# Attention scores in one plain float32 product per head, in place of three split products

## The chip, the cores and the metric

The kernel runs on one core of one Trainium2 chip. The metric is the device time of one execution in microseconds (us), lower is better. The program is one launch: an attention with mixed heads, followed by two mixtures of dense layers that read its output. A trace of one profiled execution shows, for each engine of the core, when each instruction started, how long it lasted and what its engine had waited for. TensorE is called PE (its weight loads are shown apart, as PEld), VectorE is DVE, ScalarE is ACT, GpSimd is POOL, and SyncE, which issues nearly all transfers, is SP.

## The reference

Only the first lines matter here; the rest of the program follows on the attention's output.

```python
q, k, v = float32 (4, 12, 448, 64)       # batch, heads, positions, head size
scale = 1.0 / 8.0
scores = scale * np.matmul(q, k.transpose(0, 1, 3, 2))
scores = np.einsum('bhij,hg->bgij', scores, w_pre)
scores = scores - np.max(scores, axis=-1, keepdims=True)
attn = np.exp(scores)
attn = attn / (np.sum(attn, axis=-1, keepdims=True) + 1e-09)
attn = np.einsum('bhij,hg->bgij', attn, w_post)
out = np.matmul(attn, v)
```

The output, as 1792 rows of 768, goes through a dense layer pair (768 to 2048 and back, with ELU) and then through a routed layer of 8 experts. Neither of these is touched.

## The kernel before, in words

**Tiles and steps.** `attention` works on 16 query tiles (4 batches of 448 rows, each cut into 120, 120, 120 and 88 rows). Heads go in 6 pairs p; the two heads of a pair lie on partitions 0 to 63 and 64 to 127 of the query and key tiles. The main loop (L397) has 48 steps n, three for each tile. A step mixes, exponentiates and mixes back a third of tile n // 3, multiplies a third of the tile before by the values, and makes the scores of two pairs of heads for the tile T = (n + 5) // 3, so the scores run about two tiles ahead of their use. The scores of tile 0 and of four pairs of tile 1 are made ahead of the loop.

**What each engine does in a step, in the order written.** The order of every engine is that of the program text (a manual schedule), so an instruction that waits holds up all that is behind it on its engine.

- PE: `mix_pre` twice (L204: 16 records of matmul on 64-by-64 quarters of the array), `mix_post` of the first unit of the step before (L264, 64 small matmuls), `av` (L286 and L292, 32 matmuls), `qk` for two pairs of heads (L164), `mix_post` of the second unit (64 matmuls).
- ACT: the rounded copy of the queries (`high_q`, L141), four exponentials with row sums (L225), a copy of `mix_post`'s result (L270), in some steps a rounded copy of keys (`split_k`, L135), the first head of each pair out of PSUM (L168), and two more copies (L270).
- DVE: four row maxima (L212), the remainder of the queries (`low_q`, L145), a copy (L270), the reciprocals of the row sums (L239 and L240), a copy of the `av` result (L302), the second head of each pair (L169).
- POOL: in some steps the remainder of the keys (`split_k`, L136), then the mixing weights scaled by the reciprocals (L245).
- SP: the moves of scores into the layout that mixing wants (`relayout`, L196), stores of the result, loads of queries, keys and values for later tiles (L120, L124, L129).

**The scores.** `qk(T, p)` takes two PSUM banks, one for each head, out of a ring of four (`ps_w`, shared with `mix_pre`). For the first two tiles (T < PLAIN = 2) it multiplies the queries by the keys as they were loaded, in float32. From the third tile on it uses split operands: each number as a rounded high part (float32r) and a remainder, and three products, high by high, high by low, low by high (`THREE`), summed in PSUM. In the loop's order over the three products, the two heads alternate:

```python
for i, (a, z) in enumerate(THREE if T >= PLAIN else ()):
    for ab, ps in enumerate(pss):
        rows = slice(ab * 64, (ab + 1) * 64)
        nc.tensor.matmul(out=ps[:PR, :S], lhsT=qt[T, p // 2][rows, a, p % 2, :], rhs=kt[b, p][rows, z, :],
                         start=(i == 0), stop=(i == 2))
```

**Splitting.** `high_q` and `low_q` split a third of a query tile in each step from n = 1 to n = 42. `split_k` splits the keys of one pair; it runs twice a step in steps 0 to 2 (batch 0, remainder on DVE) and in three steps for each later batch (n = 6 to 8, 18 to 20, 30 to 32, remainder on POOL): 24 times in all. The buffers: raw queries 2, raw keys 6 (one size for all pairs), split queries 3, split keys 1 for each pair.

**After the scores.** From n = 43 on no scores are made, their pools are closed, and the first parts of `mixtures` are put between the attention's last steps. Everything after some 345 us is `mixtures`.

Of the kernel before, what the change touches and what calls it, by code (L numbers as in the profile page):

```python
# [8 lines left out]
FP32 = mybir.dt.float32  # L9
FP32R = mybir.dt.float32r  # L10
# [3 lines left out]
ALU = mybir.AluOpType  # L14
# [4 lines left out]
B, H, S, D = 4, 12, 448, 64  # L19
NT, DM, DFF = B * S, H * D, 2048  # L20
NK = DM // 128
# [8 lines left out]
PR = 120  # L30
# [7 lines left out]
NA = WHOLE * H + NK  # L38
ORDER = [2 * p + (p + s) % 2 for s in range(2) for p in range(NK)]
SCALE = 1.0 / 8.0  # L40
PLAIN = 2
THREE = ((0, 0), (0, 1), (1, 0))


# [36 lines left out]
def attention(tc, q, k, v, w_pre, w_post, xT, mix, ident):  # L81
# [11 lines left out]
    nc = tc.nc  # L93
    with ExitStack() as ctx, ExitStack() as mixing, ExitStack() as scoring:
        pool = lambda name, bufs, ctx=ctx, **kw: ctx.enter_context(tc.tile_pool(name=name, bufs=bufs, **kw))
# [5 lines left out]
        x_p = pool("a_x", 3)  # L101
        d_p = pool("a_d", 1, mixing)
        s_p = [pool("a_s0", 1, scoring, side="right"), pool("a_s1", 1, mixing)]
        k_p = pool("a_k", 1, scoring, side="right")
        rk_p = pool("a_rk", 6, scoring, side="right")
        rq_p = pool("a_rq", 2, scoring, side="right")
        q_p = pool("a_q", 3, scoring, side="right")
        ps_f = pool("ps_f", 2, space=PSUM)
        ps_x = pool("ps_x", 1, space=PSUM)
        ps_w = pool("ps_w", 4, mixing, space=PSUM, side="right")  # L110

        tiles = [(b, it) for b in range(B) for it in range(len(ROWS))]
        raw_q, raw_k, vt, kt, qt, st, att = {}, {}, {}, {}, {}, {}, {}

        def load_q(T, us=None):
            b, it = tiles[T]
            if T not in raw_q:
                raw_q[T] = rq_p.tile([128, NK, PR], FP32, tag="rq", name="rq")
            for p0, p1 in us or [(0, NK)]:
                nc.sync.dma_start(out=raw_q[T][:, p0:p1], in_=q[b, :, it, p0:p1])  # L120

        def load_k(b, p):
            raw_k[b, p] = rk_p.tile([128, S], FP32, tag="rk", name="rk")
            nc.sync.dma_start(out=raw_k[b, p], in_=k[b, p])  # L124

        def load_v(b, p):

            vt[b, p] = v_p.tile([128, 2 * WHOLE + 1, D], FP32, tag=f"v{p}", name="v")
            nc.sync.dma_start(out=vt[b, p].rearrange("s r d -> s (r d)"), in_=v[b, p])  # L129

        def split_k(b, p, eng):

            t = kt[b, p] = k_p.tile([128, 2, S], FP32R, tag=f"k{p}", name="k")
            raw = raw_k.pop((b, p))
            nc.scalar.copy(out=t[:, 0], in_=raw)  # L135
            eng.tensor_tensor(out=t[:, 1], in0=raw, in1=t[:, 0], op=ALU.subtract)  # L136

        def high_q(T, u):

            t = qt[T, u] = q_p.tile([128, 2, 2, PR], FP32R, tag="q", name="qq")  # L140
            nc.scalar.copy(out=t[:, 0], in_=raw_q[T][:, 2 * u:2 * u + 2])  # L141

        def low_q(T, u):
            t = qt[T, u]
            nc.vector.tensor_tensor(out=t[:, 1], in0=raw_q[T][:, 2 * u:2 * u + 2], in1=t[:, 0], op=ALU.subtract)  # L145

        def split_q(T, u):
            high_q(T, u)
            low_q(T, u)

        def qk(T, p):

            b = tiles[T][0]
            if p == 0:
                st[T] = s_p[T % 2].tile([128, H, S], FP32, tag="s", name="s")
            pss = [ps_w.tile([128, 512], FP32, tag="w", name="qk") for _ in range(2)]
            for ab, ps in enumerate(pss):
                rows = slice(ab * 64, (ab + 1) * 64)
                if T < PLAIN:
                    nc.tensor.matmul(out=ps[:PR, :S], lhsT=raw_q[T][rows, p, :], rhs=raw_k[b, p][rows, :])  # L160
            for i, (a, z) in enumerate(THREE if T >= PLAIN else ()):
                for ab, ps in enumerate(pss):
                    rows = slice(ab * 64, (ab + 1) * 64)
                    nc.tensor.matmul(out=ps[:PR, :S], lhsT=qt[T, p // 2][rows, a, p % 2, :], rhs=kt[b, p][rows, z, :],  # L164
                                     start=(i == 0), stop=(i == 2))

            def move():
                nc.scalar.activation(out=st[T][:PR, 2 * p, :], in_=pss[0][:PR, :S], func=ACTF.Copy, scale=SCALE)  # L168
                nc.vector.tensor_scalar(out=st[T][:PR, 2 * p + 1, :], in0=pss[1][:PR, :S], scalar1=SCALE, scalar2=None,  # L169
                                        op0=ALU.mult)  # L170
            return move
# [13 lines left out]
        def relayout(U):  # L185

            dr[U] = {}
            for j, G in enumerate(U):
                T, r, m = blks[G]
                whole = ROWS[tiles[T][1]][1] // BR * BR  # L190
                t = r // BR if r < whole else (whole // BR) + (r - whole) // m
                rows = st[T][:PR].rearrange("(a t) h s -> t a h s", a=BR)[t][:m]
                t = d_all[n_d[0] % ND]
                n_d[0] += 1
                half = m // 2 * H
                nc.sync.dma_start(out=t[UP - half:UP + half, :], in_=rows)  # L196
                dr[U][0, j], dr[U][1, j] = t[:UP], t[UP:UP + HP]
# [31 lines left out]
        def softmax(U):  # L229
            for e in exps(U):  # L230
                e()
# [79 lines left out]
        def store():  # L311
            for to, x in stores:
                nc.sync.dma_start(out=to, in_=x)
            stores.clear()
# [28 lines left out]
        def when(n):  # L343

            return n // 3, n % 3


        warm = const.tile([128, 128], FP32, name="warm")
        nc.vector.memset(warm, 0.0)
        load_q(0, [(0, 2)])  # L350
        load_k(0, 0)
        load_k(0, 1)
# [15 lines left out]
        ps = ps_f.tile([128, 512], FP32, tag="f", name="f")  # L368
# [3 lines left out]
        for p in range(NK):  # L372
# [11 lines left out]
            if p == 3:  # L384
                nc.vector.tensor_copy(out=kposts[1][:HP].rearrange("p (g i) -> p g i", g=H),
                                      in_=kpost[:HP].rearrange("p (g i) -> p g i", g=H)[:, :, :HR])
# [10 lines left out]
        for n in range(NP):  # L397
            cur, old = units[n], units[n - 1] if n else ()
            new = units[n + 1] if n + 1 < NP else ()
            T, u = when(n + 5)  # L400
            T1, u1 = when(n + 6)
            T2, u2 = when(n + 7)
            for U in new[1:]:
                relayout(U)
            store()
            if n == NP - 5:
                scoring.close()
            late = n >= NP - 5
            for bp in values[:2] if n else ():
                load_v(*bp)  # L410
            del values[:2 if n else 0]
            if T2 < len(tiles):
                if u2 == 0:
                    load_q(T2)
                if tiles[T2][1] == 0:
                    load_k(tiles[T2][0], 2 * u2)
                    load_k(tiles[T2][0], 2 * u2 + 1)
            if PLAIN <= T < len(tiles):
                high_q(T, u)
            for i, U in enumerate(cur):  # L420
                mix_pre(U)
                if i == 0 and n + 2 < NP:
                    relayout(units[n + 2][0])
            for U in cur:
                top(U)
            if PLAIN <= T < len(tiles):
                low_q(T, u)
            softmax(cur[0])
            moves, scores = [mix_post(U) for U in old[:1]], []
            weighted = [av((n - 1) // 3 - 1, (n - 1) % 3)] if n >= 4 else []  # L430
            if T < len(tiles):
                scores.append(qk(T, 2 * u))
            if not late:
                for U in cur[1:]:
                    softmax(U)
            for m in moves:
                m[1](nc.scalar.copy)
                m[0](nc.vector.tensor_copy)
            if late:
                for U in cur[1:]:  # L440
                    softmax(U)
                next(mix)
            keys = (tiles[T1][0], 2 * u1, nc.gpsimd) if T1 < len(tiles) and tiles[T1][1] == 0 else ()
            if n < 3:
                keys = 0, 2 * n, nc.vector
            if keys:
                split_k(*keys)
            if late:
                next(mix)
            norm(cur)  # L450
            for f in weighted:
                f()
            if T < len(tiles):
                scores.append(qk(T, 2 * u + 1))
            for f in scores:
                f()
            if keys:
                split_k(keys[0], keys[1] + 1, keys[2])
            moves = [mix_post(U) for U in old[1:]]
            if late:  # L460
                next(mix)
            for m in moves:
                m[1](nc.scalar.copy)
                m[0](nc.scalar.copy)
            if n == NP - 1:
                av(n // 3 - 1, n % 3)()
            if late:
                next(mix)
# [903 lines left out]
```

## Time and profile before

| what | value |
|---|---|
| median of 3 runs | 1002.85 us (1000.85 to 1008.06) |
| profiled execution | 1004.38 us, of which the span of its trace is 1002.6 us |
| busy share of the span | PE 98%, weight loads 85%, DVE 72%, ACT 55%, POOL 24% |
| granted clock of TensorE over the span | 0.992 of full speed (2.4 GHz) |
| plain score products (L160), 48 records of matmul | 15.3 us busy |
| split score products (L164), 504 records of matmul | 67.0 us busy |
| mixing ahead of softmax (L204), 736 records of matmul | 166.9 us busy, in two groups that run side by side |

The span is the time from the first to the last instruction in the trace; the execution's own time is 1.78 us longer. A busy time of a group is the time in which at least one of its instructions ran, so for matmuls that run side by side it is less than count times duration. The recorded duration of a matmul includes its way through the array, so successive matmuls overlap in the records, and what one costs is read from the distance between starts.

### The profile page before, as it was taken

Reading aid. Unit: us, or ns where it says so; the run is one execution under the profiler, and the core shown is the slowest. Engines: PE = TensorE matmul, PEld = TensorE weight load, DVE = VectorE, ACT = ScalarE, POOL = GpSimd, SP = SyncE. Lnnn points to the kernel's source line nnn. Section 1 sums busy time; section 2 is a strip of 40 time slices with the busy share of each in tenths; the row PEclk is TensorE's granted clock in tenths of the full one; section 3 lists DMA queues with packets and bytes.
Section 4 is the critical chain, followed back from the end, with each engine's and each line's share of the span. In section 5 each row is a group of like instructions: output and inputs, shape, how many; then the busy total and the mean of one; then the engine's idle time right before and its main releaser. Section 6 shows DMA issues by size and latency. Waiting matters only on the chain. (4 is left out here: it accounts for less than half of the span.)

```text
span 1002.6 us, 29974 instructions
## 1 busy us (share of the span) xinstructions
PE 979.3 (98%) x12216; PEld 855.5 (85%) x12216; DVE 725.1 (72%) x1462; ACT 553.3 (55%) x1115; POOL 243.8 (24%) x290
## 2 busy tenths in 40 slices
PE   9999999999998999999999999999999999999997
PEld 4677777777776789998999999999999988889986
DVE  6877677767776786676766478786867748999962
ACT  4887688778776754445545453212122117878760
POOL 2343224225222313223323100100101004452002
PEclk9999999999999999999999999999999999999998
DMA  5674664664557575545666398533433396999800
GB/s 183 223 244 141 204 225 153 201 216 165 184 191 235 171 218 171 165 159 176 213 224 222 121 324 263 168 113 95 126 95 118 115 337 248 393 397 398 343 9 35
DMA packets 129252, 200.05 MB, mean 200 GB/s; under 512 B 32002, under 2 KB 95923, under 8 KB 128856
## 3 DMA queue, kind: packets, MB, share of 16 engines
q1 hardware_dynamic: 126824, 191.60, 56.8%
q0 software_dynamic: 2240, 6.51, 1.8%
q8 instruction: 97, 1.59, 0.7%
q14 instruction: 43, 0.35, 0.1%
q10 hardware_dynamic: 48, 0.00, 0.0%
HBM read 122.86 MB, written 37.65 MB: 160 GB/s over the span
## 5 line engine op out<-in xcount | busy, mean ns | idle before, releaser
L916 PE MATMUL o<-w,gh 128*128 128x384 f32 (+2 forms) x1344 | 238.1, 336 | 0.0
L634 PE MATMUL h<-xh,w 128*128 128x448 f32 x1152 | 235.3, 366 | 1.8 <-DVE xh L570 1.4
L916 PEld LDWEIGHTS o<-w,gh 128*128 128x128 f32 x1344 | 232.0, 188 | 2.0
L634 PEld LDWEIGHTS h<-xh,w 128*128 128x128 f32 x1152 | 215.7, 188 | 20.4 <-DVE xh L570 2.1
L212 DVE TENSOR_REDUCE nmx<-c 128x1 f32<-128x448 f32 x184 | 102.4, 617 | 51.0 <-PE c L204 50.9
L264 PEld LDWEIGHTS f<-kr,e 64*64 64x64 f32 x5888 | 104.4, 134 | 37.3 <-issue 24.1
L225 ACT ACTIVATE e<-c,nmx 128x448 f32<-128x448 f32 x184 | 114.3, 632 | 25.3 <-DVE nmx L212 25.2
L245 POOL TENSOR_SCALAR kr<-kpost,rs 128x60 f32<-128x60 f32 x184 | 79.8, 456 | 189.2 <-DVE rs L240 90.0
L803 DVE SCALAR_TENSOR_TENSOR junk<-x,wrow 128x768 f32<-128x768 f32 x117 | 111.8, 955 | 18.2 <-ACT x L946 15.8
L1084 DVE TENSOR_TENSOR wlo<-w1t,whi 128x1536 fp32r<-128x1536 f32 x64 | 111.0, 1752 | 14.0 <-ACT whi L1082 13.7
L264 PE MATMUL f<-kr,e 64*64 64x60 f32 (+1 forms) x5888 | 106.9, 218 | 4.4 <-issue 3.3
L551 POOL TENSOR_TENSOR wf<-a,p 128x768 f32<-128x768 f32 x32 | 66.1, 2064 | 181.2 <-DVE p L549 139.6
L1082 ACT CAST whi<-w1t 128x1536 fp32r<-128x1536 f32 x64 | 93.9, 1484 | 19.9 <-PE ph L1111 10.5
L788 ACT CAST gh<-gr 128x512 fp32r<-128x512 f32 x56 | 35.0, 624 | 97.7 <-PE o L916 35.5
L204 PE MATMUL c<-d,kpre_low 64*64 64x448 f32 x368 | 84.7, 545 | 0.7 <-DMA d<-s 0.7
L204 PE MATMUL c<-d,kpre_up 60*64 60x448 f32 x368 | 82.2, 545 | 0.0
L270 ACT COPY at<-f 128x420 f32<-128x420 f32 (+1 forms) x136 | 65.4, 516 | 28.7 <-PE f L264 27.9
L292 PE MATMUL xp<-at,v 128*64 128x120 f32 (+1 forms) x1152 | 68.7, 268 | 2.8 <-issue 2.6
L168 ACT ACTIVATE s<-qk 120x448 f32<-120x448 f32 x96 | 52.1, 548 | 30.0 <-PE qk L164 19.5
L851 POOL DMA_INDIRECT slots<-pairs,si x14 | 18.8, 1346 | 204.3 <-DVE si L850 156.2
L164 PE MATMUL qk<-k,qq 64*120 64x448 f32 x504 | 67.0, 389 | 0.6 <-ACT e L225 0.2
L292 PEld LDWEIGHTS xp<-at,v 128*64 128x64 f32 x1152 | 57.4, 140 | 10.5 <-issue 9.2
(189 smaller groups left out, 1329.1 us busy)
## 6 DMA issues: line engine op xcount, KB each, us to landing
w1t<-in_moe_w_dram SPq DMA_DIRECT2D x64, 768.0 KB
d<-s SPq DMA_DIRECT2D x176, 210.0 KB
gT<-g SPq DMA_DIRECT2D x64, 224.0 KB
f<-in_moe_w_in_dram SPq DMA_DIRECT2D x16, 768.0 KB
f<-in_moe_w_out_dram SPq DMA_DIRECT2D x16, 768.0 KB
gr<-gT SPq DMA_DIRECT2D x48, 256.0 KB
rq<-in_q_dram SPq DMA_DIRECT2D x15, 360.0 KB
rk<-in_k_dram SPq DMA_DIRECT2D x24, 224.0 KB
```

The source lines that it names most:

```text
L164: nc.tensor.matmul(out=ps[:PR, :S], lhsT=qt[T, p // 2][rows, a, p % 2, :], rhs=kt[b, p][rows, z, :], start=(i == 0), stop=(i == 2))
L204: nc.tensor.matmul(out=ps[j * UP:(j + 1) * UP, :S], lhsT=kpre_up[UP:UP + HP, :] if z else kpre_low, rhs=d[z, j])
L212: nc.vector.tensor_reduce(out=t, in_=c, op=ALU.max, axis=AX.X, negate=True)
L225: nc.scalar.activation(out=e, in_=c, func=ACTF.Exp, bias=t, accum_out=sms[0][:, k + i:k + i + 1])
L245: nc.gpsimd.tensor_scalar(out=kr, in0=kposts[z], scalar1=rs[:, 2 * i + z:2 * i + z + 1], scalar2=None, op0=ALU.mult)
L264: nc.tensor.matmul(out=ps[to, heads, z, :], lhsT=e[rows, keys * JW:(keys + 1) * JW], rhs=kr[rows, first * HR:(first + n) * HR])
L292: nc.tensor.matmul(out=ps[i][z * 64:(z + 1) * 64, :n], lhsT=vt[b, p][:, jc * 2 + z, :], rhs=att[T][:, jc * H + ORDER.index(2 * p + z), :n] ...
L634: nc.tensor.matmul(out=ps, lhsT=w[:, a, kk, :], rhs=xs[tb, kk][:, z, :], start=(kk == 0 and a + z == 0), stop=(kk == NK - 1 and a == 1))
L803: nc.vector.scalar_tensor_tensor(out=t[:, o:o + n], in0=x2, scalar=1.0, in1=w, op0=ALU.mult, op1=ALU.mult, accum_out=lg[:, e:e + 1])
L916: mm = nc.tensor.matmul(out=po[c][:, :cols[c].stop - cols[c].start], lhsT=gs[i][fc // GC][:, a, fc % GC, :], rhs=wo[fc][:, z, cols[c]], st ...
L1082: nc.scalar.copy(out=hi, in_=t)
L1084: nc.vector.tensor_tensor(out=lo, in0=t, in1=hi, op=ALU.subtract)
```

## The change

`qk` uses the plain product of the first two tiles for all tiles: one float32 matmul for each head, from the query and key tiles as loaded. The split, its four helper functions and the calls in the loop go, and with them the tiles for split operands. The query tile has two buffers as before, the key tiles get two buffers for each pair of heads. Loads are issued at the same places, in the same sizes.

```diff
-PLAIN = 2
 THREE = ((0, 0), (0, 1), (1, 0))
...
-        k_p = pool("a_k", 1, scoring, side="right")
-        rk_p = pool("a_rk", 6, scoring, side="right")
-        rq_p = pool("a_rq", 2, scoring, side="right")
-        q_p = pool("a_q", 3, scoring, side="right")
+        k_p = pool("a_k", 2, scoring, side="right")
+        q_p = pool("a_q", 2, scoring, side="right")
...
         def load_q(T, us=None):
             b, it = tiles[T]
-            if T not in raw_q:
-                raw_q[T] = rq_p.tile([128, NK, PR], FP32, tag="rq", name="rq")
+            if T not in qt:
+                qt[T] = q_p.tile([128, NK, PR], FP32, tag="q", name="q")
             for p0, p1 in us or [(0, NK)]:
-                nc.sync.dma_start(out=raw_q[T][:, p0:p1], in_=q[b, :, it, p0:p1])
+                nc.sync.dma_start(out=qt[T][:, p0:p1], in_=q[b, :, it, p0:p1])
 
         def load_k(b, p):
-            raw_k[b, p] = rk_p.tile([128, S], FP32, tag="rk", name="rk")
-            nc.sync.dma_start(out=raw_k[b, p], in_=k[b, p])
+            kt[b, p] = k_p.tile([128, S], FP32, tag=f"k{p}", name="k")
+            nc.sync.dma_start(out=kt[b, p], in_=k[b, p])
...
-        def split_k(b, p, eng):
-
-            t = kt[b, p] = k_p.tile([128, 2, S], FP32R, tag=f"k{p}", name="k")
-            raw = raw_k.pop((b, p))
-            nc.scalar.copy(out=t[:, 0], in_=raw)
-            eng.tensor_tensor(out=t[:, 1], in0=raw, in1=t[:, 0], op=ALU.subtract)
-
-        def high_q(T, u):
-
-            t = qt[T, u] = q_p.tile([128, 2, 2, PR], FP32R, tag="q", name="qq")
-            nc.scalar.copy(out=t[:, 0], in_=raw_q[T][:, 2 * u:2 * u + 2])
-
-        def low_q(T, u):
-            t = qt[T, u]
-            nc.vector.tensor_tensor(out=t[:, 1], in0=raw_q[T][:, 2 * u:2 * u + 2], in1=t[:, 0], op=ALU.subtract)
...
             for ab, ps in enumerate(pss):
                 rows = slice(ab * 64, (ab + 1) * 64)
-                if T < PLAIN:
-                    nc.tensor.matmul(out=ps[:PR, :S], lhsT=raw_q[T][rows, p, :], rhs=raw_k[b, p][rows, :])
-            for i, (a, z) in enumerate(THREE if T >= PLAIN else ()):
-                for ab, ps in enumerate(pss):
-                    rows = slice(ab * 64, (ab + 1) * 64)
-                    nc.tensor.matmul(out=ps[:PR, :S], lhsT=qt[T, p // 2][rows, a, p % 2, :], rhs=kt[b, p][rows, z, :],
-                                     start=(i == 0), stop=(i == 2))
+                nc.tensor.matmul(out=ps[:PR, :S], lhsT=qt[T][rows, p, :], rhs=kt[b, p][rows, :])
...
-            if PLAIN <= T < len(tiles):
-                high_q(T, u)
...
-            if PLAIN <= T < len(tiles):
-                low_q(T, u)
...
-            keys = (tiles[T1][0], 2 * u1, nc.gpsimd) if T1 < len(tiles) and tiles[T1][1] == 0 else ()
-            if n < 3:
-                keys = 0, 2 * n, nc.vector
-            if keys:
-                split_k(*keys)
...
-            if keys:
-                split_k(keys[0], keys[1] + 1, keys[2])
```

## Rows read from the trace of the kernel before

**Rows 1.** Busy time by stretch: length, PE, PEld, DVE, ACT, POOL, clock, DMA share, GB/s.
```profile
25.00:303.00 278.00, 271.88 (x7508) 205.36 (x7508) 201.45 (x456) 220.61 (x587) 86.90 (x179) 0.99 0.59 195
303.00:345.00 42.00, 36.60 (x1084) 28.39 (x1082) 28.77 (x60) 27.08 (x68) 15.47 (x24) 1.00 0.64 195
```

**Rows 2.** Waits of PE, 25 to 303 us: releaser, us in total, times, longest.
```profile
PE xp L286 <- issue: 2.6, 2, 2.3
PE f L264 <- issue: 2.1, 1, 2.1
...
PE qk L164 <- ACT e L225: 0.2, 1, 0.2
```

**Rows 3.** Timeline of PE over one step: start, length, instruction, shapes, count.
```profile
149.91 1.48 PE L164 MATMUL qk<-k,qq 64*120 64x448 f32 x12
...
152.28 0.57 PE L204 MATMUL c<-d,kpre_low 64*64 64x448 f32 x1
...
152.69 0.54 PE L204 MATMUL c<-d,kpre_low 64*64 64x448 f32 x1
...
153.06 0.54 PE L204 MATMUL c<-d,kpre_low 64*64 64x448 f32 x1
...
153.81 1.09 PE L264 MATMUL f<-kr,e 64*64 64x60 f32 x64
...
156.44 1.48 PE L164 MATMUL qk<-k,qq 64*120 64x448 f32 x12
157.85 0.34 PE L264 MATMUL f<-kr,e 64*64 64x60 f32 x8
```

**Rows 4.** Timeline of PE's weight loads in the second of these score groups.
```profile
156.95 0.18 PEld L164 LDWEIGHTS qk<-k,qq 64*120 64x120 f32 x2
...
157.15 0.18 PEld L164 LDWEIGHTS qk<-k,qq 64*120 64x120 f32 x2
```

**Rows 5.** Instructions of line 160: duration min/median/max, first and last start.
```profile
L160 PE MATMUL qk<-rk,rq x48: 536/633/1099, 4.1 to 23.1; 64*120 64x448 f32 x48
```

**Rows 6.** Timeline of weight loads in the plain products ahead of the loop.
```profile
13.16 0.49 PEld L160 LDWEIGHTS qk<-rk,rq 64*120 64x120 f32 x4 [0.40 <-DVE s L169]
14.04 0.37 PEld L160 LDWEIGHTS qk<-rk,rq 64*120 64x120 f32 x4 [0.38 <-DVE s L169]
```

**Rows 7.** Timelines of weight loads and matmuls, first mixing products of step 0.
```profile
16.97 0.19 PEld L204 LDWEIGHTS c<-d,kpre_low 64*64 64x64 f32 x2 [0.92 <-ACT s L168]
17.09 0.19 PEld L204 LDWEIGHTS c<-d,kpre_up 60*64 60x64 f32 x2
...
17.00 0.56 PE L204 MATMUL c<-d,kpre_low 64*64 64x448 f32 x1 [0.22 <-DMA d<-s]
17.13 0.56 PE L204 MATMUL c<-d,kpre_up 60*64 60x448 f32 x1
17.40 0.54 PE L204 MATMUL c<-d,kpre_low 64*64 64x448 f32 x1
```

**Rows 8.** Instructions of lines 135, 136, 141 and 145: duration min/median/max, starts.
```profile
L135 ACT CAST k<-rk x24: 557/588/604, 22.4 to 239.2; 128x448 fp32r<-128x448 f32 x24
...
L136 POOL TENSOR_TENSOR k<-rk,k x18: 1138/1142/1152, 62.6 to 241.0; 128x448 fp32r<-128x448 f32 x18
...
L141 ACT CAST qq<-rq x42: 382/400/439, 24.2 to 299.0; 128x240 fp32r<-128x240 f32 x42
...
L145 DVE TENSOR_TENSOR qq<-rq,qq x42: 393/398/400, 27.6 to 301.1; 128x240 fp32r<-128x240 f32 x42
```

**Rows 9.** Timeline of PE: the first mixing products of steps 2 and 3.
```profile
30.48 0.94 PE L204 MATMUL c<-d,kpre_low 64*64 64x448 f32 x2
...
37.51 0.94 PE L204 MATMUL c<-d,kpre_low 64*64 64x448 f32 x2
```

**Rows 10.** A stall of PE: timeline, busy time of the next 4 us, queue.
```profile
119.75 0.38 PE L286 MATMUL xp<-at,v 64*64 64x88 f32 x6 [2.25 <-issue]
...
120.00:124.00 4.00, 4.00 (x42) 3.33 (x36) 0.79 (x2) 0.48 (x1) 1.41 (x4) 0.57 0.40 131
...
q8 instruction: 97, 1.59, 0.7%
```

More of the change, by code (lines that the diff above doesn't have):

```diff
@@ L112, in attention @@
         tiles = [(b, it) for b in range(B) for it in range(len(ROWS))]
-        raw_q, raw_k, vt, kt, qt, st, att = {}, {}, {}, {}, {}, {}, {}
+        qt, kt, vt, st, att = {}, {}, {}, {}, {}
         def load_q(T, us=None):
             b, it = tiles[T]
-            if T not in raw_q:
-                raw_q[T] = rq_p.tile([128, NK, PR], FP32, tag="rq", name="rq")
+            if T not in qt:
+                qt[T] = q_p.tile([128, NK, PR], FP32, tag="q", name="q")
             for p0, p1 in us or [(0, NK)]:
-                nc.sync.dma_start(out=raw_q[T][:, p0:p1], in_=q[b, :, it, p0:p1])
+                nc.sync.dma_start(out=qt[T][:, p0:p1], in_=q[b, :, it, p0:p1])
         def load_k(b, p):
-            raw_k[b, p] = rk_p.tile([128, S], FP32, tag="rk", name="rk")
-            nc.sync.dma_start(out=raw_k[b, p], in_=k[b, p])
+            kt[b, p] = k_p.tile([128, S], FP32, tag=f"k{p}", name="k")
+            nc.sync.dma_start(out=kt[b, p], in_=k[b, p])
         def load_v(b, p):
@@ L129, in load_v @@
             nc.sync.dma_start(out=vt[b, p].rearrange("s r d -> s (r d)"), in_=v[b, p])
-        def split_k(b, p, eng):
-            t = kt[b, p] = k_p.tile([128, 2, S], FP32R, tag=f"k{p}", name="k")
-            raw = raw_k.pop((b, p))
-            nc.scalar.copy(out=t[:, 0], in_=raw)
-            eng.tensor_tensor(out=t[:, 1], in0=raw, in1=t[:, 0], op=ALU.subtract)
-        def high_q(T, u):
-            t = qt[T, u] = q_p.tile([128, 2, 2, PR], FP32R, tag="q", name="qq")
-            nc.scalar.copy(out=t[:, 0], in_=raw_q[T][:, 2 * u:2 * u + 2])
-        def low_q(T, u):
-            t = qt[T, u]
-            nc.vector.tensor_tensor(out=t[:, 1], in0=raw_q[T][:, 2 * u:2 * u + 2], in1=t[:, 0], op=ALU.subtract)
-        def split_q(T, u):
-            high_q(T, u)
-            low_q(T, u)
         def qk(T, p):
@@ L400, in attention @@
             T, u = when(n + 5)
-            T1, u1 = when(n + 6)
             T2, u2 = when(n + 7)
@@ L417, in attention @@
                     load_k(tiles[T2][0], 2 * u2 + 1)
-            if PLAIN <= T < len(tiles):
-                high_q(T, u)
             for i, U in enumerate(cur):
@@ L425, in attention @@
                 top(U)
-            if PLAIN <= T < len(tiles):
-                low_q(T, u)
             softmax(cur[0])
```

## Prediction

> **What bounds the kernel now.** The first view to read is the busy time by stretch, for the part of the span in which the split scores are made [rows 1]. From 25 to 303 us PE is busy 271.9 of 278.0 us; ACT comes next with 220.6, DVE has 201.5, POOL 86.9. The stage after it, 303 to 345 us, has no scores in it and more idle time of PE. A busy PE could still be one that waits in small pieces, so the second view is PE's own waits in that stretch [rows 2]: of the idle 6.1 us most is "issue" (2.6 and 2.1 us, three events), that is, PE had no instruction to run, and only 0.2 us of it is a wait for the exponentials (ACT e) ahead of a score product. No wait for the split operands is in the list at all. The third view is the timeline of PE over one step [rows 3]. From one group of scores to the next are 156.44 - 149.91 = 6.53 us, and in them mixing, mixing back, the product with the values and the scores follow one another without a gap. So in this stretch PE sets the pace, and what the change does to the time of the step is what it does to PE's list of work.
>
> **What a split group costs.** A step makes the scores of two pairs of heads: 2 pairs x 3 products x 2 heads = 12 matmuls. They take from 156.44 to 157.85, when the next kind of work starts: 1.41 us [rows 3]. The weight loads come in twos, one for each head, 0.20 us apart [rows 4]. So the two heads run side by side on the two halves of the array's rows (one after another, 12 matmuls of 448 columns would need 12 x 0.19 = 2.2 us at the full 2.4 GHz), and the group is 6 passes of 0.20 us and 0.21 us at its edges, where the first loads and the change to the next shape of tile aren't covered.
>
> **What a plain group will cost.** The trace has plain float32 score products in the first two tiles: 48 records of matmul [rows 5] for 12 pairs of heads, so each head's product is two matmuls (and two weight loads), not one. A step will have 2 pairs x 2 heads x 2 = 8 matmuls in place of 12. What one of them costs isn't clean in those rows, since there PE waits for PSUM, but the same kind of matmul with the same 448 columns stands in every step, in the mixing ahead of the softmax: the waves of it start at 152.69 and 153.06, and after three of them the next work starts at 153.81, so (153.81 - 152.69) / 3 = 0.373 us a pass [rows 3]. That is two periods of the 2.4 GHz clock for each of 448 columns. If the two heads of a pair run side by side again, the group is 4 passes: 4 x 0.373 + 0.21 = 1.70 us against 1.41, so 0.29 us more in each step. There are 42 such steps: 42 x 0.29 = 12.2 us.
>
> The bounds of this price. From above: in the products ahead of the loop, pair follows pair at 14.04 - 13.16 = 0.88 us [rows 6]. By that a group is 2 x 0.88 + 0.21 = 1.97 us, 0.56 more, and 42 steps give 23.5 us. But the bracket of these rows names what the loads waited for, DVE's move of an earlier score out of PSUM (s L169); in the loop all four banks are free when a group starts, so I take the 0.373 of the mixing. From below: 8 weight loads in place of 12 might leave only half of the edge, 1.49 + 0.10 = 1.59 us, 0.18 more, and 7.6 us over 42 steps. A gain I exclude for the products themselves: 4 passes of 0.373 are 1.49 us, more than the whole split group takes.
>
> Do the two heads run side by side in the plain form? Here the order in the program matters. Split, the heads alternate: a matmul of the first head, one of the second, and so on. Plain, the two matmuls of the first head come in one instruction of the program, then the two of the second. The mixing has the same order, and the start of step 0 shows how it goes [rows 7]: the loads come as two for kpre_low (16.97) and then two for kpre_up (17.09), but the matmuls start as low 17.00, up 17.13, low 17.40. The first matmul of the second product began 0.27 us before the second matmul of the first. So different halves of the rows don't wait for one another, and I expect 4 passes and not 5.
>
> The Trainium skill speaks against this: "TensorE: Matmul & The Clock Gate", Part 3, section "The mechanism", says that weight loads may be pulled ahead, but that matmuls keep strict program order in start and end. By that rule the second head's first matmul could not start before the first head's second, a group would be 5 passes, and it would cost 0.37 us more in each step than I reckon; the rows of step 0 disagree with it, though they are few. What it would make of the time is a rival below.
>
> **What goes.** ACT loses 24 copies of keys at 0.588 and 42 of queries at 0.400 us: 14.1 + 16.8 = 30.9 us. DVE loses 42 x 0.398 = 16.7 us and six remainders of keys in the first steps, POOL 18 x 1.142 = 20.6 us [rows 8]. I price nearly all of it at nothing: PE's own work covers it, since ACT, the busiest of the three, has 57 us to spare in the stretch, and PE waited 0.2 us for its exponentials. What would have to be true for a gain is that PE waits, and it does so only in the first steps, which have no product with the values to cover the exponentials and in which the keys of batch 0 are split. Step 2 takes 37.51 - 30.48 = 7.03 us [rows 9], 0.5 more than a full step although it has less work. I take 0.5 us back in each of steps 1 and 2, and 0.4 us in all for steps 1 to 3, since there the longer first pair falls into the wait ahead of the second: 1.4 us.
>
> **What moves.** No transfer changes its size, its count or its place on SP's queue, so nothing on it is moved past anything. A query load for tile T goes out in step 3T - 7, into the buffer that the scores of tile T - 2 left in step 3T - 9, two steps before; a key load goes into the buffer of the batch before last. Neither waits. A wait on PE is not added either: after the group, PE has the second half of mixing back (from 149.91 + 1.41 = 151.32 to 152.28, 0.96 us) before mixing wants the PSUM banks of the scores again, as now, and the moves follow each pair's end as now. ACT and DVE are lighter then.
>
> **The sum.** 12.2 - 1.4 = 10.8 us more. Against the profiled execution: 1004.38 (span 1002.6) goes to 1015.2 (span 1013.4). That execution stood 1.5 us above the median of the runs shown, 1002.85, so on the median I forecast 1002.85 + 10.8 = 1013.6 us. What is behind the attention only starts later. About 1% is what a measurement of this kernel can tell from no change: 1012.9 us is the border, and the forecast lies just beyond it.
>
> **The rivals.**
>
> *The stalls of code loading go away (not slower).* In the stretch PE stood still for 2.25 us in one place with nothing to run [rows 10], and afterwards its granted clock was 0.57 on the mean over 4 us, that is, mostly at 1.2 in place of 2.4 GHz: 2.25 + 4 x 0.43 = 4.0 us. There is one more of the kind (the 2.1 us of mixing back in rows 2). PE's code comes in by a queue of 97 packets [rows 10], and with 8 fewer records (4 loads, 4 matmuls) in each of 42 steps the borders of the packets fall elsewhere against the transfers that delay them. If both stalls go, 8.0 us come back: 1013.6 - 8.0 = 1005.6 us, within 1% of before. It decides where both packets come in time. For it: two stalls in 42 steps are few, so they depend on phase. Against it: a border falls in nearly every step, and the steps with much traffic stay. A new stall would cost the same 4.0 us the other way.
>
> *Heads one after another in part.* If matmuls start in the order of the program, a group has a fifth pass: 0.373 x 42 = 15.7 us more, 1013.6 + 15.7 = 1029.3 us. For it: the order written. Against it: rows 7, and the four passes of the mixing in rows 3, which hold 16 matmuls.
>
> *The passes go at the pace of the first tiles.* PSUM's emptying, 0.88 us a pair, would hold in the loop too: 23.5 - 1.4 = 22.1 us more, 1024.9 us. It would need the four banks to be late when the group starts.
>
> *The relief is worth more (faster).* If ACT's 30.9 us lay on the path, the sum would turn over: 12.2 - 30.9 = 18.7 us less, 984.2 us. PE's 6.1 idle us leave no room for it, so it could hold only if the trace's busy PE were not at work.
>
> **How the numbers follow.** Forecast with its own range of 1009 to 1018 us (0.18 to 0.40 us a step and small shifts of the stalls): 0.65. Stalls gone, or one of them: 0.17. Fifth pass: 0.08. Pace of the first tiles: 0.06. Relief: 0.04. The border of 1012.9 us cuts the forecast near its middle, a little on the upper side: 0.40 of its 0.65 above, 0.25 below. So slower 0.40 + 0.08 + 0.06 = 0.54, and, rounded up for a new stall, 0.55; faster 0.04; same the rest, 0.41. The range goes from 1004 (both stalls gone) to 1023 us (close to the pace of the first tiles, or a new stall or two), and leaves out the fifth pass and the relief.
>
> **What would show it right or wrong.** Right: a group of scores in the loop has 8 records of matmul in the timeline, and takes 1.65 to 1.75 us to the start of the mixing back; full steps are 6.8 us apart; PE still has no wait for ACT or DVE in its list; steps 1 and 2 shorter than 7 us; from 345 us on the same lengths as before. Wrong: starts of the second head only after both of the first (a group near 2.07 us); a wait for s L168 or s L169 ahead of the mixing; or a step that is no longer than 6.53 us although its group is. The total is wrong with every step right if the stalls named "issue" come to another sum than in rows 2.

## The result and the profile after

The changed kernel takes 1010.97 us (median of 20 runs), the kernel before 1002.62 us (20 runs). The ratio of the means, without one run of the kernel before that took 2851.85 us, is 1.0088 with a 95% interval of 1.0063 to 1.0114, that is 6 to 11 us more, where 10.8 us were forecast. The profiled execution of the changed kernel has a span of 1011.0 us.

The busy time by stretch, of the kernel after, answers to [rows 1]:

```profile
25.00:303.00 278.00, 273.39 (x7205) 184.97 (x7200) 183.20 (x401) 196.06 (x511) 65.08 (x158) 1.00 0.58 192
```

ACT, DVE and POOL lost 25, 18 and 22 us in this stretch, and PE is busier than before. It is still the engine that sets the pace, as its waits from 25 to 315 us show (releaser, us, times, longest), against [rows 2]:

```profile
PE xp L263 <- issue: 2.3, 3, 1.6
PE f L235 <- issue: 1.2, 4, 0.6
PE xp L257 <- issue: 0.7, 1, 0.7
PE c L175 <- ACT s L139: 0.3, 1, 0.3
```

The timeline of PE over one undisturbed step, against [rows 3]:

```profile
155.82 1.77 PE L136 MATMUL qk<-k,q 64*120 64x448 f32 x8
157.51 1.13 PE L235 MATMUL f<-kr,e 64*64 64x60 f32 x64
...
162.63 1.77 PE L136 MATMUL qk<-k,q 64*120 64x448 f32 x8
164.33 0.87 PE L235 MATMUL f<-kr,e 64*64 64x60 f32 x44
```

A group has 8 records in place of 12, and the next kind of work starts 164.33 - 162.63 = 1.70 us after it; before it was 1.41. From group to group are 162.63 - 155.82 = 6.81 us, before 6.53. Both are the forecast numbers. The records of the line itself (duration min/median/max, starts) show the same instructions as [rows 5]:

```profile
L136 PE MATMUL qk<-k,q x384: 536/536/647, 4.1 to 306.7; 64*120 64x448 f32 x192
L136 PEldq EVENT_SEMAPHORE  x35: 51/51/51, 3.9 to 290.9; - x35
```

They now have a median of 536 ns, not 633. The 633 belonged to that one profile: in two more profiles of the kernel before the median is 536 ns as well. In the first, 15 of the 48 records, all begun in the first 10.6 us, took 704 to 1099 ns (why, is not shown; the granted clock reads 1.00 there), and the others of some 633 ns are products whose weight load began at the same moment as they did.

Since single executions differ by several us, both kernels were profiled three times in all (two more each, told below). This table splits the spans at the steps' starts, taken from the timelines of PE's weight loads (a step starts with the first load of mixing). "Shortest" adds up, over steps 4 to 42, the shortest step of the same kind (same place in the batch) in that profile; "excess" is what the steps took beyond it. A kind has only three or four steps in a profile, and the shortest of them can itself hold a stall; against the shortest of each kind in all three profiles of a kernel, the two rows differ by +10.7 and -5.3.

| us | before, three profiles | mean | after, three profiles | mean | difference |
|---|---|---|---|---|---|
| to step 0 | 17.0, 14.7, 14.7 | 15.5 | 15.2, 14.9, 14.8 | 15.0 | -0.5 |
| steps 0 to 3 | 27.2, 27.3, 27.2 | 27.2 | 26.3, 25.5, 26.6 | 26.1 | -1.1 |
| steps 4 to 42, shortest | 248.7, 249.6, 248.2 | 248.9 | 259.0, 260.2, 260.8 | 260.0 | +11.1 |
| steps 4 to 42, excess | 11.6, 15.3, 13.1 | 13.3 | 7.5, 6.1, 9.3 | 7.6 | -5.7 |
| steps 43 to 46 | 26.4, 28.2, 27.9 | 27.5 | 28.1, 27.0, 26.6 | 27.2 | -0.3 |
| step 47 to the end | 671.8, 671.4, 672.3 | 671.8 | 674.9, 681.7, 672.3 | 676.3 | +4.5 |
| span | 1002.6, 1006.5, 1003.5 | 1004.2 | 1011.0, 1015.2, 1010.4 | 1012.2 | +8.0 |

So the forecast cost is there, +10.7 to +11.1, and the first steps give 1.1 back. Two parts that were not in the sum nearly cancel: the stalls inside the steps became shorter, and the part behind the attention became longer in two of the three profiles. The experiments ask whether these readings hold.

### The profile page after: what moved, and what is told of

Same layout as the page of the kernel before. It is cut to its first block, busy times and chain, and to the rows that moved or that the text cites. A ratio compares the mean times of both kernels' runs of the same rounds, so it can differ in the third digit from the quotient of the medians.

```text
span 1011.0 us, 29488 instructions
## 1 busy us (share of the span) xinstructions
PE 984.1 (97%) x12048; PEld 839.3 (83%) x12048; DVE 711.6 (70%) x1414; ACT 531.9 (53%) x1049; POOL 213.4 (21%) x272
## 5 line engine op out<-in xcount | busy, mean ns | idle before, releaser
L1043 DVE TENSOR_TENSOR wlo<-w1t,whi 128x1536 fp32r<-128x1536 f32 x64 | 111.1, 1752 | 15.5 <-ACT whi L1041 15.2
L136 PE MATMUL qk<-k,q 64*120 64x448 f32 x384 | 88.9, 563 | 1.7 <-DMA k<-in_k_dram 1.6
L175 PE MATMUL c<-d,kpre_low 64*64 64x448 f32 x368 | 82.6, 545 | 0.5 <-ACT s L139 0.3
L140 DVE TENSOR_SCALAR s<-qk 120x448 f32<-120x448 f32 x96 | 59.4, 623 | 17.6 <-PE qk L136 7.6
```

The source lines that it names most:

```text
L136: nc.tensor.matmul(out=ps[:PR, :S], lhsT=qt[T][rows, p, :], rhs=kt[b, p][rows, :])
L175: nc.tensor.matmul(out=ps[j * UP:(j + 1) * UP, :S], lhsT=kpre_up[UP:UP + HP, :] if z else kpre_low, rhs=d[z, j])
L1043: nc.vector.tensor_tensor(out=lo, in0=t, in1=hi, op=ALU.subtract)
```

## The experiments

**Is PE's order of matmuls what it was taken for?** In the changed kernel the products of a step were put in another order, first heads of both pairs first:

```diff
+            for ab in range(2):
+                rows = slice(ab * 64, (ab + 1) * 64)
+                for i in range(2):
+                    nc.tensor.matmul(out=pss[i][ab][:PR, :S], lhsT=qt[T][rows, 2 * u + i, :], rhs=kt[b, 2 * u + i][rows, :])
```

> The changed kernel with the order of the plain products turned in the loop from tile 2 on: the first heads of both pairs, then the second heads of both. Theory (each half of the array's rows takes its matmuls in its own order and doesn't wait for the other half): the group stays 4 passes, 1.70 us, and the time that of the changed kernel, about 1011 us. Rival (matmuls start in program order): the second heads start only with the last matmul of the first heads, 7 passes, 7 x 0.373 + 0.21 = 2.82 us a group, 42 x 1.12 = 47 us more, about 1058 us.

Measured: 1012.2 us (before in the same runs 1001.1; ratio 1.0107, 1.0078 to 1.0137). The timeline of PE:

```profile
165.80 1.77 PE L137 MATMUL qk<-k,q 64*120 64x448 f32 x8
167.51 1.13 PE L253 MATMUL f<-kr,e 64*64 64x60 f32 x64
...
172.63 1.77 PE L137 MATMUL qk<-k,q 64*120 64x448 f32 x8
174.33 0.87 PE L253 MATMUL f<-kr,e 64*64 64x60 f32 x44
```

The group takes 1.70 to 1.71 us in this order too, not 2.82. (Steps 13, 25 and 37 take 7.1 to 7.3 us here, against 6.5 in the changed kernel; what made them longer was not looked into.) Matmuls for the two halves of the array's rows don't wait for one another, though four of one half stand ahead of the other's in the program. The rule of program order in the Trainium skill ("TensorE: Matmul & The Clock Gate", Part 3, "The mechanism") doesn't describe this chip in this use; the measurement decides.

**Is the helpers' relief worth anything?** From both sides: the changed kernel with the split work put back into tiles that nothing reads (e1), and the kernel before with the split work done only once (e2).

```diff
+            if 2 <= T < len(tiles):
+                high_q(T, u)
...
+            if keys:
+                split_k(*keys)
```

> The changed kernel with the split work put back: ACT, DVE and POOL make the rounded copies and remainders at their old places, into tiles that nothing reads; the scores stay plain. Theory (PE's passes alone set the step; the helpers' relief is worth only the 1.4 us of steps 1 to 3): 1.0 to 1.5 us above the changed kernel, so 1011 to 1013 us where before stands at 1002.6, a full step 6.8 us, a score group 1.70 us. Rival (the helpers' relief paid back a good part of the longer passes, which is why 8.4 us and not 10.8 were measured): 1014 us or more, and PE waits for ACT or DVE in its list.

Measured: 1010.7 us against 1001.1 in the same runs, ratio 1.0097 (1.0062 to 1.0131); the changed kernel had 1.0088. PE's waits from 25 to 315 us, all of them:

```profile
PE xp L273 <- issue: 1.7, 2, 1.0
PE xp L279 <- issue: 0.4, 2, 0.2
PE f L251 <- issue: 0.3, 1, 0.3
```

No wait for ACT or DVE has come back, a full step takes 6.82 us again, and only steps 0 to 3 are longer: 27.4 us, as before, against 25.5 to 26.6 in the changed kernel. So the relief is worth nothing in full steps, and in the first steps 1.3 us (27.4 against the mean of 26.1).

```diff
-                    nc.tensor.matmul(out=ps[:PR, :S], lhsT=qt[T, p // 2][rows, a, p % 2, :], rhs=kt[b, p][rows, z, :],
+                    nc.tensor.matmul(out=ps[:PR, :S], lhsT=qt[PLAIN, p // 2][rows, a, p % 2, :], rhs=kt[0, p][rows, z, :],
...
-            if PLAIN <= T < len(tiles):
+            if T == PLAIN:
                 high_q(T, u)
```

> The kernel before with three split products as now, but the split work done only once (keys of batch 0, queries of tile 2); all later tiles multiply those same operands, so later scores are left out and repeated ones stand in. Takes the helpers' work away and leaves PE's list. Theory: a full step stays 6.53 us, a score group 1.41 us, the time stays within 1.5 us of before (1001 to 1003). Rival (ACT's 26 us or POOL's 20 us lay on the path): 998 us or less, full steps under 6.45 us.

Measured: 1002.4 us, ratio 1.0015 (0.9989 to 1.0041): nothing gained. The total alone would not show it, since the repeated scores change what follows: step 47 to the end took 675.7 us in its profile, against 671.4 to 672.3 before, and steps 4 to 42 had less excess, 8.9 us. The pace of the steps does: the shortest of them add up to 248.3 us, as before. Two of its score groups start 165.14 - 158.61 = 6.53 us apart:

```profile
158.61 1.48 PE L164 MATMUL qk<-k,qq 64*120 64x448 f32 x12
...
165.14 1.48 PE L164 MATMUL qk<-k,qq 64*120 64x448 f32 x12
```

**Does the number of passes set the step?** The kernel before with two, and with one, of the three products.

```diff
-            for i, (a, z) in enumerate(THREE if T >= PLAIN else ()):
+            for i, (a, z) in enumerate(THREE[:2] if T >= PLAIN else ()):
```

> The kernel before without the third split product (remainder of the queries by high keys), so one term of the scores is left out; all split work stays. Theory (the number and pace of passes set the step): the group is 4 passes of 0.20 and 0.21 us at the edges, 1.01 us, a full step 6.13 us, 42 x 0.40 = 16.8 us less, about 986 us. Rival (ACT, with up to 6.6 us of work in steps that split keys, is as near a bound as PE): the steps that split keys stay at 6.5 us, and the gain is 13 us or less; or none, where ACT sets all steps.

Measured: 993.8 us against 1001.1, ratio 0.9918 (0.9887 to 0.9950): 5 to 11 us less, about half of what the list of PE would give. The timeline:

```profile
149.90 1.07 PE L164 MATMUL qk<-k,qq 64*120 64x448 f32 x8
150.90 1.13 PE L264 MATMUL f<-kr,e 64*64 64x60 f32 x64
...
156.02 1.06 PE L164 MATMUL qk<-k,qq 64*120 64x448 f32 x8
157.01 1.13 PE L264 MATMUL f<-kr,e 64*64 64x60 f32 x64
```

The group takes 1.00 us and the step 6.12, as expected by the theory, in steps that split keys too (steps 19, 20, 31 and 32 are 6.12 to 6.14; 18 and 30 hold stalls). So the rival's number came out, by another cause. The shortest steps add up to 238.2 us, 10 to 11 less than before, where 39 times 0.40 would be 15.6. In part that is the step with an 88-row tile, which went from 6.27 to 6.59, where PE's weight loads wait for POOL's scaled weights ("PEld f <- POOL kr", 0.69 us in step 11); the first four steps of a batch gained only 0.1 to 0.2 us each. And a wait of 7.1 us stands in the first expert, of which more below; how often it stands there in the timed runs, the profile doesn't say.

```diff
-            for i, (a, z) in enumerate(THREE if T >= PLAIN else ()):
+            for i, (a, z) in enumerate(THREE[:1] if T >= PLAIN else ()):
...
-            eng.tensor_tensor(out=t[:, 1], in0=raw, in1=t[:, 0], op=ALU.subtract)
...
-                low_q(T, u)
```

> The kernel before with the high by high product alone: the two remainder terms of the scores are left out, and with them the remainders on DVE and POOL; the rounded copies on ACT stay. Theory (passes on PE set the step until another chain does; with two products the smallest of the full steps came to 6.11 us, but the step with the 88-row tile went up from 6.27 to 6.59, waiting for POOL's scaled weights, and the stalls of code loading stayed): a score group of 2 x 0.20 + 0.21 = 0.61 us, full steps of at best 5.7 us, 33.6 us less by PE's list alone, of which half or less arrives: 985 to 992 us. Rival (PE's list alone): about 969 us. Second rival (something else already sets the step with two products): 994 us as with two.

Measured: 989.7 us against 1000.7, ratio 0.9901 (0.9868 to 0.9934). A group takes 0.60 us. A further 0.40 us off the group gave at best 0.27 us a step (5.85 after 6.12), and only 4.3 us on the sum of the shortest steps (233.9 after 238.2): below about 6.1 us the step is no longer PE's alone, and PE's list of waits has 2.1 us for ACT's moves of scores. Both are faster than either of the two kernels compared here, but they leave terms of the scores out.

**Where do the stalls come from?** First, does the excess repeat? Both kernels were profiled again.

> The kernel before, profiled once more. Theory (the stalls of code loading differ from execution to execution): the undisturbed steps repeat at 6.52 to 6.54 us, the two long steps 15 and 27 (10.3 and 10.1 us) don't repeat at that length in both places, and the excess over undisturbed steps in steps 4 to 42, 11.6 us in the first profile, differs by 2 us or more. Rival (they belong to the place in the program): steps 15 and 27 again at 10 us, excess within 1 us.

> The changed kernel, profiled once more. Theory: undisturbed full steps at 6.82 us and groups at 1.70 us again, and an excess in steps 4 to 42 that differs from the 7.5 us of the first profile by 2 us or more, or sits in other steps. Rival: the same steps with the same lengths, excess within 1 us.

Measured: the excess of before came to 15.3 us (and 13.1 in the third profile), so it varies; that of after came to 6.1, within 1.5 us of the first and mostly in the same steps. But for the long steps the theory fell. In all three profiles of before, steps 15 and 27 are among the longest (10.3, 11.0, 10.6 and 10.1, 10.1, 7.6 us), and in step 15 the stall is at the same instruction as in [rows 10]. The timeline of before, third profile:

```profile
119.84 0.38 PE L286 MATMUL xp<-at,v 64*64 64x88 f32 x6 [2.52 <-issue]
```

In the three profiles of after, both steps take 6.4 to 6.9 us. So the long stalls belong to the program, and the change took them away. For these two steps the rival of the prediction that the stalls of code loading go, with 8.0 us, came true: 7.3 us less on the mean of three profiles, against the shortest step of the kind. The stalls of the other steps took some 2 us of it back. The busy time of 8 us at the same place, first before, then after (the last columns are granted clock, DMA share and GB/s):

```profile
116.00:124.00 8.00, 5.75 (x116) 4.74 (x108) 3.98 (x10) 3.70 (x11) 1.64 (x4) 0.79 0.58 176
```

```profile
116.00:124.00 8.00, 8.00 (x251) 5.84 (x243) 5.76 (x13) 5.78 (x16) 1.65 (x4) 1.00 0.85 276
```

Before, PE stood for 2.25 us and then worked for some 4 us at a mean granted clock of 0.57 [rows 10]; after, it doesn't stop and the clock stays at 2.4 GHz.

Second, which traffic is behind the stalls? The changed kernel without the loads of keys and values after batch 0:

```diff
-                if b + 1 < B and it == len(ROWS) - 1:
+                if False:
                     values.append((b + 1, p))
...
-                if tiles[T2][1] == 0:
+                if False:
                     load_k(tiles[T2][0], 2 * u2)
```

> The changed kernel without the loads of keys and values of batches 1 to 3; all batches use those of batch 0, so their own scores and values are left out. Theory (the stalls of PE named issue are code arriving late behind these transfers; they sit in steps 6, 16, 18, 20, 26, 28, 32, 39, 40, near the key loads of steps 5 to 7, 17 to 19, 29 to 31 and the value loads of steps 14 to 16, 26 to 28, 38 to 40): the sum over steps 4 to 42 falls from 266.5 us to within 2 us of the 259.0 that its undisturbed steps add up to, and the time by 5 to 7 us, to some 1005. Rival (code loading is late without these transfers too): steps 4 to 42 stay above 264 us and the time at 1011.

Its time can't be compared: 1075 us, since the repeated keys and values give other rows to the experts, and its trace has 12,244 records of matmul where the changed kernel has 12,048, the 196 more of them in the routed layers at its end. Steps 4 to 42 took 262.3 us, between the two expectations (excess 3.3 us, against 6.1 to 9.3). PE's waits from 25 to 310 us are down from 4.2 to 0.9 us:

```profile
PE xp L263 <- issue: 0.6, 1, 0.6
PE f L235 <- issue: 0.3, 1, 0.3
```

The other two profiles of the changed kernel have 3.2 and 4.6 us of waits named issue there, and e1, with all loads, 2.4. So these loads lengthen the stalls; how much of them needs the loads, one profile doesn't say. They are not the only cause: just behind this window, in step 44, e6 has a stall of 2.3 us without them.

Third, is it the place of the code's borders? Tiny products ahead of the first score move all borders of PE's code, in before (36 products) and in after (28):

```diff
+        for _ in range(36):
+            nc.tensor.matmul(out=ps[:8, :8], lhsT=warm[:, :8], rhs=warm[:, :8])
```

> The kernel before with 36 tiny products (144 records on PE) put ahead of its first score, nothing else; they start the work some us later, so steps are compared and not the total. The stalls of steps 15 and 27 came at the same instruction in both profiles of before; PE's code comes in pieces of some 252 records, and 144 more records move the border out of that place. Theory (the place of the border against the traffic makes the long stalls): steps 15 and 27 fall from 10.3 and 10.1 us below 8 us, the excess of steps 4 to 42 from 11.6 and 15.3 us below 9. Rival (these steps are slow whatever the border): both again at 9.5 us or more.

> The changed kernel with 28 tiny products (112 records on PE) ahead of its first score. By step 15 the change has taken 14 x 8 = 112 records out, so these put the border back to where it stood in that step before; in step 27 it stays 96 records off. Theory (border): step 15 goes up from 6.6 us to 9 us or more, step 27 stays under 8. Rival (lighter traffic or lighter helpers keep the code in time): step 15 stays under 7.5 us.

Measured: in before, step 15 fell to 6.5 and step 27 to 7.2 us, and the excess to 7.4 (10.1 against the shortest steps of the three profiles of before, so not clearly under the 9 that were expected). Here is PE at the place of the stall, without a gap (timeline of before with borders moved):

```profile
120.58 0.40 PE L286 MATMUL xp<-at,v 64*64 64x88 f32 x6
120.91 1.13 PE L292 MATMUL xp<-at,v 128*64 128x88 f32 x24
121.97 1.48 PE L164 MATMUL qk<-k,qq 64*120 64x448 f32 x12
```

But in the changed kernel the border put back brought nothing back: step 15 took 6.7, step 27 7.1 us.

The kept traces tell why. Count PE's records in order: matmuls, weight loads and the semaphore records of its queue. All 151 stalls named issue (over 0.15 us, 20 to 345 us, the 14 profiles of this case) come just before a record number of the form 193 + 256 k, and each ends 0.9 to 1.7 us after a packet of 16,384 bytes on the queue q8 has ended. So these are the borders of PE's code, in pieces of 256 records, and PE stands still where the next piece is late. For the border of step 15 (record 5313) the traces give:

| run | the packet starts after PE passed the border before, us | PE's time for the 256 records up to this border, us | stall, us |
|---|---|---|---|
| before, three profiles | 3.0, 3.7, 3.3 | 3.2 | 2.3, 3.0, 2.5 |
| e2, split work done once | 1.9 | 3.1 | 1.2 |
| e8, changed, border back | 0.5 | 3.2 | none |
| changed, three profiles | 2.4, 3.1, 2.8 | 5.6 to 5.7 | none |
| e1, changed, split work back | 2.9 | 5.6 | none |
| e4, two products | 2.3 | 4.5 | none |

Two things must meet: a late packet, and a piece that PE finishes quickly: in before, 217 of its 256 records are the short ones of mixing back. In the changed kernel the packet is nearly as late as before, but 8 records less a step have moved the borders, only 150 of the 256 are mixing back, and the piece takes 5.6 us. It isn't the lighter helpers: e1 has their work back and no stall, e2 has PE's list of before without their work and still stands still at this record. e8 brought the short piece back (221 of mixing back), but there the packet came early, so what was expected of it failed. In step 27 the pieces of before and of the changed kernel take about as long (4.3 and 4.7 us), and it is the packet that starts earlier: 0.8 to 1.5 us after the border, against 4.3, 4.3 and 2.6. There too e2, without the helpers' work, stalls as before (2.4 us). So in before it is enough to move the borders to end the long stall of step 15 (e7), and in the changed kernel the 8 records less moved them. What makes a packet late at one border and not at another stays open.

**Is the longer part behind the attention due to the change?** In the first two profiles of after, and in none of before, PE waits in the first expert. PE's waits there, second profile of after:

```profile
PE y L1083 <- DVE ht L1060: 7.2, 1, 7.2
```

DVE was itself held up by POOL's small transfers. POOL's timeline, first before, then after:

```profile
831.91 0.61 POOL L1202 DMA_DIRECT2D ids<-slots  x1 [1.43 <-DMA slots<-pairs,si]
...
834.80 2.08 POOL L1089 DMA_INDIRECT xg<-x2d,ids  x1 [0.30 <-issue]
```

```profile
842.53 0.61 POOL L1161 DMA_DIRECT2D ids<-slots  x1 [4.17 <-DMA slots<-pairs,si]
...
848.26 1.01 POOL L1048 DMA_INDIRECT xg<-x2d,ids  x1 [3.14 <-DMA ids<-slots]
```

The scatter and the reads of the lists took 1.4 us and no wait worth a row in the one, 4.2 and 3.1 us in the other. The busy time of the stretch just ahead of the first of these rows shows the difference (again DMA share and GB/s at the end), before and after:

```profile
829.91:831.91 2.00, 2.00 (x16) 1.87 (x16) 0.47 (x1) 0.79 (x2) 0.57 (x1) 0.97 0.01 0
```

```profile
840.53:842.53 2.00, 2.00 (x10) 1.66 (x9) 2.00 (x5) 1.10 (x2) 0.00 (x0) 1.00 1.03 306
```

In the one the DMA engines were idle, in the other the next large weight loads had already been issued. The timelines of SP show it (before, then after):

```profile
834.40 2.02 SPq L1071 DMA_DIRECT2D w1t<-in_moe_w_dram  x2
```

```profile
837.58 7.71 SPq L1030 DMA_DIRECT2D w1t<-in_moe_w_dram  x6
```

Before, the loads are issued 2.5 us after the first read of the lists, here 4.9 us ahead of it. A third profile of each:

> The kernel before, a third profile, for the part behind the attention. In the two profiles of before PE never waits in the first expert's second product; in the two of the changed kernel it waits there 2.3 and 7.2 us (put down to DVE's ht), behind small transfers by POOL that land late when the large weight loads have begun. Theory (the change moves this wait in): no wait of over 1 us there, and 671 to 672 us from step 47 to the end. Rival (chance of the execution): a wait of 2 us or more here too.

> The changed kernel, a third profile. Theory (the change moves the wait in the first expert in): 2 us or more again, and over 674 us from step 47 to the end. Rival (chance): no such wait. In both cases undisturbed full steps of 6.82 us, groups of 1.70 us, and steps 15 and 27 without a stall of over 2 us.

Measured: no such wait in either, and 672.3 us from step 47 to the end in both. So the rival holds for the third profile of after: the part behind the attention is the same when the weight loads start late (1.0 us after the first read of the lists). The wait also came in e3 (1.8 us), e4 (7.1) and e7 (1.7), and not in e1, e2, e5 and e8; e4 and e7 have the score products of before, so it isn't bound to the plain ones. In all profiles but that of e6, with its other rows, it goes by the issue of the weight loads: no wait where they are issued 1.0 to 2.5 us after the first read of the lists, 1.7 to 2.3 us where both come within 0.3 us, and 7.1 and 7.2 us where the loads come 4.9 us ahead. Whether the change makes it more frequent, three profiles don't tell.

## Why the prediction was right

- *What bounds the stage.* PE's list, as read from [rows 1 to 3]. Shown by e1 and e2: the helpers' 31, 17 and 21 us [rows 8] are worth nothing in full steps, put back or taken away.
- *The price of a pass.* 0.373 us, taken from the mixing's waves in the same rows, was right: groups of 1.70 us where 1.70 was forecast, 0.29 us in a full step and 0.27 on the mean of steps 4 to 42 (10.7 us over 39 steps). The upper bound by [rows 6], 0.88 us a pair, belonged to products that waited for PSUM; the lower one, half an edge saved by fewer weight loads, didn't come either: in the trace of the changed kernel the passes of a group start 0.47, 0.38 and 0.38 us apart and the next kind of work 0.47 us after the last, so the edges, 0.1 us each, are at the first pass and the last, and inside the group no load is uncovered.
- *Two heads side by side.* Right, as [rows 7] had it, and settled by e3: the fifth pass, 15.7 us, is not there in any order.
- *First steps.* The relief was priced rightly, the longer groups too high. The forecast was 1.4 us less for the helpers and 3 x 0.29 = 0.9 more for the longer groups, together 0.5 less; the profiles show 1.1 less, and 1.8 in the second one (25.5 us). By e1 the relief is 1.3 us, as forecast (27.4 to 26.1), but the longer groups cost these steps 0.2 (27.2 to 27.4), not 0.9.
- *Sum.* 10.8 forecast; 11.1 - 1.1 = 10.0 found in these two parts, or 9.6 with 10.7. The measured 6 to 11 us hold the forecast, but near the upper end; the median stays under the border of 1012.9 us, on the side to which the prediction gave 0.41 and not the 0.55 of the other. What the sum left at zero were the stalls: on the mean of three profiles 5.7 us less, the most of it the two long ones in steps 15 and 27. That was priced as a rival at 8.0 us and 0.17. The prediction took those stalls for a matter of phase that might as well grow; they were fixed places of the program that the change happened to clear. Against it stands the longer part behind the attention, 4.5 us on the mean of the same profiles and most of it the wait in the first expert, of which the prediction knew nothing: "what is behind the attention only starts later" didn't hold in two of three. That these two nearly cancel is luck.
- *No wait added.* Right in full steps, but for 0.2 us in one. The wait that the prediction names as a sign of being wrong, for a score's move out of PSUM (ACT s) ahead of the mixing, is however in the list of two of the three profiles, 0.3 us in the first and 0.7 us in the third. All but 0.2 us of it stands at the start of step 2, and step 1 took 7.1 and 7.4 us there, not under 7 us as was said, and 6.3 in the second profile, which has no such wait.

## What to carry to other kernels

When one engine sets the pace, price a change by that engine's list alone, in passes read from starts of neighbouring instructions of the same shape, even of another line: three passes of 0.20 us are cheaper than two plain float32 ones of 0.37 us each, whatever three idle helpers save. Before a stall is put down to chance, profile the same kernel again: one that returns at the same instruction belongs to the program, and inserting a few harmless instructions ahead tells whether the place of the code is part of it, and counting the engine's records up to each stall tells whether the places are borders of its code. A term of a few us that only one profile shows should go into the range, with its sign open.

## What the runs showed that was not expected

Two long stalls of PE in before, with the slow clock after them some 4 us each, vanish when 144 records of work without effect are put ahead; steps 4 to 42 then take 258.3 us, 3.9 less than the mean of before. The start comes 3 us later by the added work (step 0 at 17.7 against 14.7 us), and the one run of that kernel took 1004.5 us beside 1004.0 of before, so next to nothing is left of it. And the length of the routed layers depends, by up to 10 us (671.4 to 681.7 us from step 47 to the end), on whether a few small transfers get through before the large weight loads start again: 7.2 of these 10 us are the wait itself.
